# Holding back loads until the second chunk's transpose has landed, in a cross-covariance attention and maxout FFN kernel

## The chip, the cores and the metric

The kernel runs on one core of a Trainium2 chip. The metric is device time in microseconds of that core. A profile's span is some 2 us shorter than the time of the same execution (before: 584.5 of 586.35). GpSimd issues the loads, which cast float32 to bf16 or fp8, into one queue (q0); SyncE issues the DMA transposes and the stores (q1). The profile counts both queues against the same 16 DMA engines. A load or transpose "lands" when its completion is signalled; "the queue is dry" means that no load packet is left to move; "rings" are these queues on the DMA engines. In profile lines PE is TensorE, POOL GpSimd and SP SyncE; v_sb is a v tile, vt_sb its transpose, wo_sb the output weight, h_ps and o_ps what the matmuls for h and for the output write.

## The reference, cut to what matters

```python
# 4 batches; q, k, v: (4, 6144, 256)
qn, kn = q / norm(q, axis=1), k / norm(k, axis=1)
a = softmax(kn.T @ qn / tau)            # 256 x 256 per batch
x = (v @ a).reshape(24576, 256)
h = max(x @ w1, x @ w2, x @ w3)         # 24576 x 768
out = h @ w_out
```

The kernel folds `a` into w1, w2, w3 once per batch, so that each 512-row chunk of v, transposed, needs 36 matmuls for h (128x512) and 24 for the output (128x256). There are 12 chunks per batch, 48 in all, numbered from 0 here; "the second chunk" is chunk 1.

## The kernel before

```python
v_pool = ctx.enter_context(tc.tile_pool(name="v", bufs=5))
...
# issued by GpSimd, in this order, after batch 0's k and q:
load_w(0)
load_v(0)
load_w(1)
load_v(1)
wo_sb = consts.tile([P, FC, d_model], BF16, name="wo_sb")
POOL.dma_start(out=wo_sb, in_=moe_w_out.rearrange("(fc p) d -> p fc d", p=P))
load_v(2)
...
def v_transpose(gi):                    # 256 KB of bf16, through the DMA engines
    v_sb = v_tiles.pop(gi)
    SP.dma_start_transpose(out=vt_tile(gi), in_=v_sb.rearrange("p t c -> p (t c)"))
def v_transpose_pe(gi):                 # the same on TensorE, two copies out of PSUM
    ...
aw_half(et, rinv, aw, 0, [2], lambda: v_transpose_pe(0))
v_transpose(1)

load_v(3)
for b in range(B):
    ...
    for ch in range(NCH):
        gi = b * NCH + ch
        load_v(gi + 4)
        v_transpose(gi + 2)
        if more and 1 <= ch < 9:        # the next batch's k and q, six groups at a time
            load_k(b + 1, (ch - 1) * 6, 6)
            load_q(b + 1, (ch - 1) * 6, 6)
        ...                             # h blocks of this chunk, output of the one before
```

The v tiles have five buffers. Chunk 5's load (v5) takes v0's, and v6 takes v1's: GpSimd must wait with v6 until v1's transpose has read v1. The kernel keeps each engine's instructions in program order (its `keep_order`).

## Time and profile before

| | before |
|---|---|
| time, median | 586.0 us (584.98 to 586.59, 4 runs) |
| span of the profile | 584.5 us |
| TensorE busy | 557.8 us, 95% |
| TensorE's longest wait in chunk work | 4.98 us before chunk 1 |
| granted clock over the span | 0.993 |

The table says that the kernel is a stream of matmuls, with one place in the chunk work where it stops for data. Two groups of the page's list of DMA issues give the normal cost of what is disputed (columns: issues, KB each, median us from issue to landing):

```profile
v_sb<-in_v_dram POOLq DMA_DIRECT2D x48, 256.0 KB, 4.0
...
vt_sb<-v_sb SPq DMA_TRANSPOSE x47, 3.7
```

And GpSimd's timeline shows what it issued behind v1, and where it stopped (start us, length us, what; in brackets its idle time before, and what ended it):

```profile
36.47 0.83 POOL L135 DMA_DIRECT2D wo_sb<-in_moe_w_out_dram  x1 [0.35 <-DMA w_sb<-in_moe_w_dram]
...
42.59 0.53 POOL L102 DMA_DIRECT2D q_sb<-in_q_dram  x1 [0.44 <-DMA w_sb<-in_moe_w_dram]
56.57 0.53 POOL L110 DMA_DIRECT2D v_sb<-in_v_dram  x1 [13.46 <-DMA vt_sb<-v_sb]
```

v6 waited 13.46 us for the transpose of v1.

### The profile page before, as it was taken

Reading aid. Unit: us, or ns where it says so; the run is one execution under the profiler, and the core shown is the slowest. Engines: PE = TensorE matmul, PEld = TensorE weight load, DVE = VectorE, ACT = ScalarE, POOL = GpSimd, SP = SyncE. Lnnn points to the kernel's source line nnn. Section 1 sums busy time; section 2 is a strip of 40 time slices with the busy share of each in tenths; the row PEclk is TensorE's granted clock in tenths of the full one; section 3 lists DMA queues with packets and bytes.
Section 4 is the critical chain, followed back from the end, with each engine's and each line's share of the span. In section 5 each row is a group of like instructions: output and inputs, shape, how many; then the busy total and the mean of one; then the engine's idle time right before and its main releaser. Section 6 shows DMA issues by size and latency. Waiting matters only on the chain.

```text
span 584.5 us, 9286 instructions
## 1 busy us (share of the span) xinstructions
PE 557.8 (95%) x3316; PEld 327.9 (56%) x3316; DVE 405.5 (69%) x623; ACT 305.6 (52%) x526; POOL 225.3 (39%) x232
## 2 busy tenths in 40 slices
PE   2786999999999999999999999999999999999997
PEld 2652555555575555555575555555575555555554
DVE  0035678778748787777848778777857777778775
ACT  0033357676735447767646446767745444444442
POOL 4241017877671006777770105777671000000000
PEclk9998899999999999999999999999999999999999
DMA  8999927988468635888649624899646344323211
GB/s 77 107 171 163 140 56 135 141 122 155 89 118 120 105 101 94 156 131 134 124 87 145 108 83 99 125 155 133 119 91 127 73 90 117 82 58 106 55 72 73
DMA packets 75134, 64.83 MB, mean 111 GB/s; under 512 B 52304, under 2 KB 61392, under 8 KB 75088
## 3 DMA queue, kind: packets, MB, share of 16 engines
q0 software_dynamic: 18400, 26.75, 38.8%
q1 hardware_dynamic: 56544, 37.23, 24.9%
q8 instruction: 26, 0.43, 0.3%
q10 hardware_dynamic: 144, 0.26, 0.1%
q14 instruction: 20, 0.16, 0.1%
HBM read 78.64 MB, written 25.17 MB: 178 GB/s over the span
## 4 chain that ended last, share of the span: by engine, by line
PE 90%; DMA 9%; POOL 1%; issue 0%; DVE 0%; POOLq 0%
PE h_ps L320 63%; PE o_ps L339 21%; DMA q_sb<-in_q_dram 3%; PE gram L226 3%; DMA vt_sb<-v_sb 2%; PE ew_ps L273 2%; DMA k_sb<-in_k_dram 2%; DMA v_sb<-in_v_dram 1%; PE o_ps L359 0%; POOL w_sb L128 0%; POOL k_sb L99 0%; PE n_ps L207 0%; PE n_ps L209 0%; DVE o_sb L365 0%; POOL ident masks.py:199 0%
## 5 line engine op out<-in xcount | busy, mean ns | idle before, releaser
L320 PE MATMUL h_ps<-vt_sb,aw_sb 128*128 128x512 bf16 x1728 | 409.0, 381 | 5.0 <-DMA vt_sb<-v_sb 5.0
L324 DVE TENSOR_TENSOR s_mx<-h_ps,s_mx 128x512 bf16<-128x512 f32 x288 | 197.8, 687 | 105.8 <-ACT s_mx L323 98.7
L320 PEld LDWEIGHTS <-aw_sb 128*128 128x128 bf16 x1728 | 168.8, 98 | 169.9 <-DMA vt_sb<-v_sb 5.5
L323 ACT ACTIVATE s_mx<-h_ps 128x512 bf16<-128x512 f32 x288 | 171.4, 595 | 138.8 <-PE h_ps L320 137.5
L325 DVE TENSOR_TENSOR ht_sb<-h_ps,s_mx 128x512 bf16<-128x512 f32 x288 | 199.3, 692 | 30.7 <-DVE s_mx L324 0.5
L195 POOL TENSOR_TENSOR acc<-acc,sq 128x768 f32<-128x768 f32 x90 | 147.5, 1650 | 70.8 <-ACT sq L189 70.6
L339 PE MATMUL o_ps<-wo_sb,ht_sb 128*128 128x256 bf16 x1128 | 154.0, 273 | 0.0
L339 PEld LDWEIGHTS <-ht_sb 128*128 128x128 bf16 x1128 | 110.5, 98 | 53.3 <-issue 0.6
L342 ACT ACTIVATE o_sb<-o_ps 128x512 f32<-128x512 f32 x94 | 56.1, 597 | 83.0 <-PE o_ps L339 83.0
L110 POOL DMA_DIRECT2D v_sb<-in_v_dram x48 | 26.7, 559 | 105.3 <-DMA vt_sb<-v_sb 101.6
L189 ACT ACTIVATE sq<-q_sb 128x768 bf16<-128x768 fp8e4 x48 | 40.5, 844 | 0.0
L189 ACT ACTIVATE sq<-k_sb 128x768 bf16<-128x768 fp8e4 x48 | 40.1, 835 | 0.0
L192 POOL CAST acc<-sq 128x768 f32<-128x768 bf16 x6 | 4.9, 820 | 74.7 <-ACT sq L189 74.7
L102 POOL DMA_DIRECT2D q_sb<-in_q_dram x32 | 17.6, 553 | 12.4 <-DMA k_sb<-in_k_dram 11.0
L157 PE MATMUL kk<-k_sb 128*128 128x256 fp8e4 x48 | 7.8, 339 | 13.6 <-DMA k_sb<-in_k_dram 13.6
L99 POOL DMA_DIRECT2D k_sb<-in_k_dram x31 | 17.0, 551 | 1.0 <-POOLq L439 0.8
L273 PE MATMUL ew_ps<-w_sb,et 128*128 128x384 bf16 x96 | 17.1, 326 | 0.0
L276 ACT ACTIVATE aw_sb<-ew_ps,rinv 128x384 bf16<-128x384 f32 x24 | 13.8, 581 | 6.1 <-PE ew_ps L273 5.1
L226 PE MATMUL gram<-k_sb,q_sb 128*128 128x512 fp8e4 x144 | 16.8, 276 | 0.0
L226 PEld LDWEIGHTS <-q_sb 128*128 128x256 fp8e4 x144 | 15.9, 136 | 0.6
L178 ACT ACTIVATE lnk<-kb_ps 128x256 f32<-128x256 f32 x1 | 0.4, 384 | 27.6 <-PE kb_ps L175 27.6
L157 PEld LDWEIGHTS <-k_sb 128*128 128x256 fp8e4 x48 | 6.5, 182 | 14.7 <-DMA k_sb<-in_k_dram 14.7
(49 smaller groups left out, 107.7 us busy)
## 6 DMA issues: line engine op xcount, KB each, us to landing
out_dram<-o_sb SPq DMA_DIRECT2D x47, 512.0 KB, 2.9
v_sb<-in_v_dram POOLq DMA_DIRECT2D x48, 256.0 KB, 4.0
k_sb<-in_k_dram POOLq DMA_DIRECT2D x24, 192.0 KB, 5.5
q_sb<-in_q_dram POOLq DMA_DIRECT2D x24, 192.0 KB, 7.0
k_sb<-in_k_dram POOLq DMA_DIRECT2D x5, 256.0 KB, 11.1
q_sb<-in_q_dram POOLq DMA_DIRECT2D x5, 256.0 KB, 19.4
w_sb<-in_moe_w_dram POOLq DMA_DIRECT2D x6, 192.0 KB, 8.9
vt_sb<-v_sb SPq DMA_TRANSPOSE x47, 3.7
```

The costliest lines, as they stand in the source:

```text
L102: POOL.dma_start(out=qk[b][0][:, g0:g0 + w, :], in_=q_r[b][:, g0:g0 + w, :])
L110: POOL.dma_start(out=t, in_=v_r[gi // NCH, gi % NCH])
L189: ACT.activation(out=sq, in_=src, func=AF.Square)
L195: POOL.tensor_tensor(out=acc, in0=acc, in1=sq, op=ALU.add)
L226: PE.matmul(g[:, j * C:(j + 1) * C], lhsT=qt[:, tsl, j * P:(j + 1) * P], rhs=kt[:, tsl, :], start=(tp == 0 and j == 0), stop=(tp == NG // ...
L273: PE.matmul(ew[:, :FH], lhsT=et[:, j, ic * P:(ic + 1) * P], rhs=w_sb[m][:, j, fsl], start=(j == 0), stop=(j == CC - 1))
L320: PE.matmul(t.rearrange("p (t n) -> p t n", t=TPC), lhsT=aw[m][:, ic, fsl], rhs=vt[:, :, ic, :], start=(ic == 0), stop=(ic == CC - 1))
L323: ACT.activation(out=s_mx, in_=hp[0], func=AF.Copy)
L324: DVE.tensor_tensor(out=s_mx, in0=hp[1], in1=s_mx, op=ALU.max)
L325: DVE.tensor_tensor(out=ht[:, fc, :], in0=hp[2], in1=s_mx, op=ALU.max)
L339: PE.matmul(st["ps"][:, half], lhsT=ht[:, fc, t * P:(t + 1) * P], rhs=wo_sb[:, fc, :], start=(fc == 0), stop=(fc == FC - 1))
L342: ACT.activation(out=st["o"][:, t - 1:t + 1, :].rearrange("p t d -> p (t d)"), in_=st["ps"], func=AF.Copy)
```

## The change

Its intent: TensorE waits 5 us for chunk 1's transpose, which shares the DMA engines with loads that nobody needs yet. So those loads are put behind a guard, a one-column copy on GpSimd that reads the transposed tile and so waits for its landing.

```diff
     load_v(1)
     wo_sb = consts.tile([P, FC, d_model], BF16, name="wo_sb")
-    POOL.dma_start(out=wo_sb, in_=moe_w_out.rearrange("(fc p) d -> p fc d", p=P))
-    load_v(2)
...
     v_transpose(1)
+    guard = consts.tile([P, 1], BF16, name="guard")
+    POOL.tensor_copy(out=guard, in_=vts[1][:, TPC - 1, CC - 1, P - 1:P])
+    POOL.dma_start(out=wo_sb, in_=moe_w_out.rearrange("(fc p) d -> p fc d", p=P))
+    load_v(2)
     load_v(3)
```

## The prediction

> **What bounds the kernel now.** I read the page first. TensorE is busy 95% of the 584.5 us span, and the chain that ended last is 90% TensorE and 9% DMA, so the steady part is a matmul stream that loads do not limit. The change touches only the start, so I next read the chain of waits in order of time there, then TensorE's timeline.
>
> The chain of waits, window 0 to 110 us (start us, length us, what):
> ```profile
> 35.54 8.08 DMA v_sb<-in_v_dram
> 43.63 12.41 DMA vt_sb<-v_sb
> 56.09 5.30 PE h_ps L320 x12
> ```
> The second chunk's v load is issued at 35.54 and lands at 43.63. Its transpose, issued then, lands only at 56.05, 12.4 us later. The page gives 3.7 us as the median of all 47 transposes: some 8.7 us are contention.
>
> TensorE, timeline from 44 us:
> ```profile
> 44.47 6.64 PE L320 MATMUL h_ps<-vt_sb,aw_sb 128*128 128x512 bf16 x30
> 56.09 1.46 PE L320 MATMUL h_ps<-vt_sb,aw_sb 128*128 128x512 bf16 x3 [4.98 <-DMA vt_sb<-v_sb]
> ```
> The first chunk ends at 51.11 and TensorE waits 4.98 us. It also comes back slow: 3 matmuls in 1.46 us, where 30 took 6.64. The per-microsecond table shows why (columns: window, length, busy time of PE, PEld, DVE, ACT, POOL, granted clock, DMA share, GB/s):
> ```profile
> 53.00:54.00 1.00, 0.00 (x0) 0.00 (x0) 0.00 (x0) 0.00 (x0) 0.00 (x0) 1.00 1.19 144
> 54.00:55.00 1.00, 0.00 (x0) 0.00 (x0) 0.00 (x0) 0.00 (x0) 0.00 (x0) 0.83 1.55 75
> ...
> 60.00:61.00 1.00, 1.00 (x4) 0.36 (x3) 0.35 (x1) 0.32 (x1) 0.00 (x0) 0.50 1.06 100
> 61.00:62.00 1.00, 1.00 (x8) 0.69 (x7) 0.90 (x2) 0.00 (x0) 0.00 (x0) 0.76 1.03 100
> 62.00:63.00 1.00, 1.00 (x7) 0.48 (x5) 0.14 (x1) 0.38 (x1) 0.00 (x0) 1.00 1.13 109
> ```
> The clock is half from 54.65 (0.83 of one microsecond: 0.65 full, 0.35 half) to 61.5. TensorE works in that state from 56.09 to about 61.48, 5.4 us, and loses half of it: 2.7 us. **The gap costs 4.98 + 2.7 = 7.7 us**, 1.3% of the time. That is all this change can win.
>
> Last, what the rings carried while the transpose waited (q0: loads from GpSimd; q1: SyncE's transposes), window 48 to 49, then 55.5 to 57.5:
> ```profile
> q0 software_dynamic: 94, 0.18, 96.0%
> q1 hardware_dynamic: 95, 0.02, 17.8%
> ```
> ```profile
> q1 hardware_dynamic: 1922, 0.48, 116.1%
> ```
> In company the two queues pass packets one for one, 94 to 95. Alone, the transposes pass 961 a microsecond. A transpose is 256 KB in 256-byte packets, 1024 of them; a v load is 128 packets of 2 KB, a k or q piece 128 of 1.5 KB (from the tile shapes and the trace's packet sizes). So **a transpose needs 1024 load packets to go by, or the load queue to run dry**. Before, it is the latter: the load queue was drained at about 53.6 apart from stragglers, and the transpose landed 2.4 us later.
>
> **What the Trainium skill says.** "DMA: Bandwidth & Descriptors", Queues, rings and completion order: each DMA engine round-robins between the queue rows that have work, at packet granularity. The trace agrees (94 to 95). Same page, Anatomy of one DMA: about 2 us fixed per DMA. The trace agrees in kind: a v load's median is 4.0 us to landing for about 1.3 us of data. "TensorE: Matmul & The Clock Gate", Part 1: after an idle window of about 3.4 us the clock halves; it returns after a busy one; the window runs free. The trace agrees: the half-rate stretch, 54.65 to 61.48, is 6.8 us, two such windows.
>
> **The change, part by part.** No engine's order changes except GpSimd's: one 128x1 copy is added, and the output weight and v2 move behind it.
>
> (a) Removed: no load is issued between v1's (35.54) and the guard. v1 lands at about 43.6 as before, since those loads were behind it in one queue. Its transpose then has free rings: 43.63 + 3.7 = 47.3, before TensorE needs it at 51.11. The 4.98 us gap and its 2.7 us slow stretch go: **-7.7 us**, a kernel of 578.8 if nothing came in their place.
>
> (b) Added: the copy, some 0.2 us (128x1 memsets at the start took 0.10), on an idle GpSimd. Then the output weight is issued at about 47.6.
>
> (c) Moved: the DMA engines fall idle until about 48.9 (issue to first packet was 1.2 us for the v load issued at 56.57). Queued after that, in order: output weight, v2, v3, v4, v5, k, q, v6, k, q. Before, GpSimd stopped ahead of v6 until 56.57, because v6 takes v1's buffer and so waits for v1's transpose. Now that transpose has landed and v6, k, q follow at once. From 46 to 48 only loads ran, at 0.40 MB in 2 us: 1.97 us for the output weight (393 KB) and 1.31 for a v load (262 KB). From 10 to 20, 107 GB/s with fp8 k and q: 1.84 us for 197 KB, about 1.9 beside transposes. Sums: output weight 50.9; v2 52.2; v3, v4, v5 56.1; k, q 59.9; v6 61.2; k, q **65.0**. I add 0.6 for the slow start seen at 58 us.
>
> The output weight lands near 52; its first use, after two blocks of chunk 1 (2 x 1.29 us past 51.11), is 53.7. A thin margin, no wait.
>
> v2 lands at about 53.3 and its transpose is issued then. Ahead of it in time stand v3 to the last q: at most 8 loads x 128 = 1024 packets, fewer once its own first packet has gone out (1.7 us after issue in the steady part, 3.9 under load). So it cannot finish before the queue is dry: 65.6 plus the 2.4 us tail of before, **about 68.0**. Chunk 2 needs it at 51.11 + 36 x 0.216 + 24 x 0.109 = 61.5 (the rates of the chain: 18 in 3.88 us, 6 in 0.66). **A new gap of about 6.5 us, one chunk later.** It is long enough to hold an idle clock window, so the clock halves again: +1.7 to 3.4 us by phase, 2.6 in the middle.
>
> (d) The sum: 586.5 - 7.7 + 6.5 + 2.6 = 587.9. A check by another way: before, chunk 2 began at 67.84 + 1.29 = 69.13; now at 68.0 and 2.6 slower: +1.5, giving 588.0.
>
> **The rivals.**
> 1. *The gap just goes*: v2's transpose is quick or in time, 578.8 to 580. For it: the third and fourth transposes of before were harmless. Against: they had the long gap to finish in, and one for one sharing is what the windows show.
> 2. *The gap moves and shrinks*: the transpose lands at 63 to 66, the clock halves or not by phase, 581 to 586. It needs k, q and v6 to be issued later than I think; nothing but GpSimd's limit of eight loads in flight (the output weight waited for the first weight load, eight before it, by the releasers) holds them, and the last k and q need only the output weight and v2 landed.
> 3. *The gap moves and grows*: slower start, longer tail, transpose at 70, full slow stretch: 590 to 592.
> 4. *The output weight becomes the wait* at 53.7: with 1.7 us of margin at most a microsecond or two, and it would take the same from the later gap, since that one ends at an absolute time.
> GpSimd does not become the bound: it sat idle from 43 to 56.
>
> **Range and chances.** My point is **588.0 us**. 584 to 592 takes in a transpose landing from 65 to 70 and the clock's phase. Even the full gain, 578.8, is 1.3%, so faster by over 2% gets 0.01; slower by over 2% (598.2) needs ten more microseconds than I find: 0.02; within 2%: 0.97.
>
> **What would show it.** Right: vt_sb of the second chunk lands at about 47.3; no TensorE wait near 51; a wait on vt_sb of 5 to 8 us near 61.5; half clock behind it; equal packet counts of both queues between 57 and 65; the next v load (v7) only at about 68. Wrong: no wait at 61.5, more transpose than load packets in company, a wait of the output matmuls on wo_sb at 53.7, or the last k and q issued only after 60.

## The result, and the profile after

The changed kernel takes 587.13 us (586.58 to 587.61, 4 runs) against 586.0. The ratio is 1.0021, interval 1.0001 to 1.0041: within 2%, and slightly slower; a repeat in later rounds gave 1.0024, 1.0011 to 1.0037. Ratios here are the mean time of one kernel's fast runs over that of the other's of the same rounds, so not quite the ratio of the medians.

The chain of waits after, from v1's load on (start us, length us, what):

```profile
35.60 8.07 DMA v_sb<-in_v_dram
43.67 0.02 issue
43.69 2.80 DMA vt_sb<-v_sb
46.49 0.06 issue
46.55 0.19 POOL guard L380
46.73 0.04 issue
46.78 0.82 POOL wo_sb L381
47.60 6.23 DMA v_sb<-in_v_dram
53.83 0.02 issue
53.85 14.24 DMA vt_sb<-v_sb
68.09 0.05 issue
68.13 4.08 PE h_ps L318 x12
```

This is to be read against the three lines of before. Chunk 1's transpose took 2.80 us in place of 12.41: the rings were indeed free. But the chain does not go to TensorE from there. It goes through the guard to v2's load and v2's transpose, and that one took 14.24 us, longer than the one that was cured. TensorE's timeline says the same:

```profile
44.55 9.23 PE L318 MATMUL h_ps<-vt_sb,aw_sb 128*128 128x512 bf16 x42
53.61 0.82 PE L337 MATMUL o_ps<-wo_sb,ht_sb 128*128 128x256 bf16 x6
...
68.13 4.08 PE L318 MATMUL h_ps<-vt_sb,aw_sb 128*128 128x512 bf16 x12 [6.56 <-DMA vt_sb<-v_sb]
```

The 42 h matmuls run from chunk 0 into chunk 1 without a stop, and the output weight, first used at 53.61, is there. Then, one chunk later, TensorE waits 6.56 us. GpSimd's timeline shows that the stop at the v1 buffer has become a stop at v2's, three loads further on:

```profile
50.76 0.60 POOL L110 DMA_DIRECT2D v_sb<-in_v_dram  x1
52.80 0.54 POOL L99 DMA_DIRECT2D k_sb<-in_k_dram  x1 [1.44 <-DMA wo_sb<-in_moe_w_out_dram]
54.12 0.53 POOL L102 DMA_DIRECT2D q_sb<-in_q_dram  x1 [0.78 <-DMA v_sb<-in_v_dram]
68.62 0.53 POOL L110 DMA_DIRECT2D v_sb<-in_v_dram  x1 [13.97 <-DMA vt_sb<-v_sb]
```

The packets of both queues, window 57 to 66 us:

```profile
q0 software_dynamic: 643, 0.95, 96.8%
q1 hardware_dynamic: 588, 0.15, 13.2%
```

In nine microseconds the transposes passed 588 of the 1024 packets that one needs, nearly one for each load packet. From 66.3 on, with the load queue all but dry, they passed 1145 in 1.7 us, those of v3's transpose among them. Sharing is not the whole of the 14.24 us: by the packet records the first transpose packet moved only at 57.68, 3.8 us after the issue, where chunk 1's, with nothing beside it, took 1.3 us (43.69 to 44.97). And the half clock returned, a little shorter in effect than before (columns as in the prediction):

```profile
64.00:65.00 1.00, 0.00 (x0) 0.00 (x0) 0.00 (x0) 0.00 (x0) 0.00 (x0) 0.50 1.12 117
...
69.00:70.00 1.00, 1.00 (x4) 0.42 (x3) 0.00 (x0) 0.60 (x1) 1.00 (x3) 0.50 1.10 339
70.00:71.00 1.00, 1.00 (x5) 0.33 (x3) 0.77 (x2) 0.00 (x0) 0.21 (x1) 0.58 1.30 224
71.00:72.00 1.00, 1.00 (x6) 0.46 (x5) 0.62 (x1) 0.60 (x1) 0.00 (x0) 1.00 1.19 141
```

The clock is back at about 70.8, so TensorE works 2.7 us at half speed, and loses 1.3 us (before: 5.4 and 2.7). The account: before lost 4.98 + 2.7 = 7.7 us, after loses 6.56 + 1.3 = 7.9. That fits the two profiled executions, 584.5 and 584.8 us; the medians are 1.1 us apart, and the other executions of the two were not traced.

### The profile page after: what moved, and what is told of

Its sections match the earlier page's. It is cut to its first block, busy times and chain, and to the rows that moved or that the text cites. A ratio compares the mean times of both kernels' runs of the same rounds, so it can differ in the third digit from the quotient of the medians.

```text
span 584.8 us, 9287 instructions
## 1 busy us (share of the span) xinstructions
PE 556.3 (95%) x3316; PEld 327.3 (56%) x3316; DVE 405.4 (69%) x623; ACT 305.6 (52%) x526; POOL 225.7 (39%) x233
## 4 chain that ended last, share of the span: by engine, by line
PE 88%; DMA 10%; POOL 1%; issue 0%; DVE 0%; POOLq 0%
PE h_ps L318 61%; PE o_ps L337 21%; DMA q_sb<-in_q_dram 3%; DMA vt_sb<-v_sb 3%; PE gram L224 3%; DMA v_sb<-in_v_dram 2%; PE ew_ps L271 2%; DMA k_sb<-in_k_dram 2%; PE o_ps L357 0%; POOL w_sb L128 0%; POOL k_sb L99 0%; PE n_ps L205 0%; PE n_ps L207 0%; POOL wo_sb L381 0%; DVE o_sb L363 0%
```

## The experiments

The theory: once its first packet moves, a transpose passes one packet for each load packet, so it lands only when enough load packets have gone by or the load queue is dry; the guard merely moved the transpose that meets the full queue. The rivals: v2's transpose is late because v2 was issued late; or the output weight is what matters in either gap. All kernels give the right result. Unless it says otherwise, an edit is to the changed kernel.

### Two by two: which of the two moved loads matters

Either load goes back in front of the guard alone, then both do.

```diff
 e1_wo_before                       e2_v2_before
     wo_sb = consts.tile(...)           wo_sb = consts.tile(...)
+    POOL.dma_start(out=wo_sb, ...) +   load_v(2)
     ...                                ...
     POOL.tensor_copy(out=guard, ...)   POOL.tensor_copy(out=guard, ...)
-    POOL.dma_start(out=wo_sb, ...)     POOL.dma_start(out=wo_sb, ...)
     load_v(2)                      -   load_v(2)
     load_v(3)                          load_v(3)

 e3_guard_before_v3: both edits, so only load_v(3) and later stay behind the guard
```

> Only v2 and later loads stay behind the guard; the output weight goes back in front. Theory (the new wait at chunk 2 comes from the loads queued behind v2, packet for packet): the output weight has passed before the second chunk's transpose starts, which still lands by 47.5 us; the load queue is dry some 2 us sooner than in the changed kernel, v2's transpose lands at about 66, the gap before chunk 2 is 4 to 5 us instead of 6.6: 584 to 586 us. Rival (holding back the output weight is what counts in either gap): the first gap of 5 us comes back, or the second goes: 579 or 586 with a wait near 51.

Measured: 586.01 us (584.38 to 586.27), ratio to before 0.9995. In the profile chunk 1 had no wait, v2's transpose took 14.42 us and landed at 65.81, and the gap before chunk 2 was 4.46 us. The place of the output weight shifts the gap by about the 2 us that the weight's own load takes, and does not make or cure it. The profiled execution was the quickest of four; the others, at 586.0 to 586.3, had a granted clock of 0.993 against its 0.995, which fits a longer half-rate stretch; they were not traced.

> Only the output weight and v3 and later stay behind the guard; v2 goes in front. Theory: v2's transpose follows the first one directly and both land by 51 us, no wait before chunk 1 or 2; the third chunk's transpose now stands against the queue (output weight to the k and q behind v7) and lands near 72, when it is needed: gap of 0 to 1 us, 578.5 to 580. Rival (any load issued close behind v1 slows its transpose as before): a wait of 2 us or more near 51, above 582.

Measured: 580.07 us (578.76 to 580.52), ratio 0.9896, just above my range. No wait before chunk 1 or 2; what is left is 1.05 us before chunk 3, at 72.99, and 0.19 us for the output weight at 53.58. The guard still holds that weight, which landed 7.1 us after its issue here (5.7 in the changed kernel).

> Output weight and v2 both back in front, the guard alone stays, ahead of v3. Theory: 56 load packets per engine more behind v1 have passed by 46 us, both transposes land by 51, v3's near 70, before 72: no wait on a transpose at all, 578.5 to 579.5, better than both kernels. Rival (the output weight and v2 behind v1 made the first gap): wait of several us near 51, 583 or more.

Measured: 579.46 us (579.25 to 579.5), ratio 0.9888, interval 0.9874 to 0.9903. The output weight and v2 right behind v1, which the change had taken for the culprits, did chunk 1's transpose little harm: it landed at 47.99, 4.24 us after its issue. So most of the 12.41 us of before came from v3 and the loads after it. Here are v3's own transpose, from the chain of waits, and TensorE's one wait on a transpose in this profile, where I had expected none:

```profile
54.16 18.20 DMA vt_sb<-v_sb
...
72.41 2.76 PE L320 MATMUL h_ps<-vt_sb,aw_sb 128*128 128x512 bf16 x12 [0.40 <-DMA vt_sb<-v_sb]
```

v3's transpose took 18.20 us, longer than the one that was cured, but it was needed only at about 72: the contention is still there, moved to where there is time for it.

So what matters is on which side of the guard v2 stands: with it behind, some 586 to 587 us; in front, 579 to 580. The output weight's place is worth about 1 us. The rival about the output weight falls. But v2 in front is also v2 early, so these three do not yet tell the queue from the late issue.

### A second guard: does a free ring for v2's transpose cure it?

```diff
     load_v(2)
+    v_transpose(2)
+    guard2 = consts.tile([P, 1], BF16, name="guard2")
+    POOL.tensor_copy(out=guard2, in_=vts[2][:, TPC - 1, CC - 1, P - 1:P])
     load_v(3)
...
-            v_transpose(gi + 2)
+            if gi > 0:
+                v_transpose(gi + 2)
```

> The changed kernel with a second guard: v3 and later wait for v2's transpose as well. Theory: v2's transpose lands near 57 and chunk 2 starts without a wait, but v3 then starts at 57, its transpose stands against v4 to the k and q behind v7 and lands near 78, needed at 72: the gap moves on to chunk 3, 5 to 7 us, 584 to 588. Rival (v2's transpose was late because v2 was; a free ring for it is the cure): no gap left, 579.

Measured: 589.22 us (588.47 to 590.49), ratio 1.0058, the slowest of all. The chain of waits from chunk 1's transpose on:

```profile
43.82 3.15 DMA vt_sb<-v_sb
...
53.71 3.10 DMA vt_sb<-v_sb
...
60.67 19.49 DMA vt_sb<-v_sb
80.17 0.05 issue
80.21 3.88 PE h_ps L318 x9
```

This is the cleanest picture of the mechanism. Two guards make two transposes quick, 3.15 and 3.10 us, and the next, the first without one, takes 19.49. v2 was issued at 48.08, no earlier than in the changed kernel (47.60), and its transpose was quick and in time: the rival about v2's late issue falls. The gap went on to chunk 3, at 8.13 us rather than the 5 to 7 that I expected, and the time came 1 us above my range; I had taken the transpose to land near 78, and it landed at 80.16.

### A shorter queue, and smaller packets

```diff
 e5_kq_later
-            if more and 1 <= ch < 9:
-                load_k(b + 1, (ch - 1) * 6, 6)
-                load_q(b + 1, (ch - 1) * 6, 6)
+            if more and 2 <= ch < 10:
+                load_k(b + 1, (ch - 2) * 6, 6)
+                load_q(b + 1, (ch - 2) * 6, 6)

 e8_small_packets: the first two pieces of k and of q take every second group of twelve
-                load_k(b + 1, (ch - 1) * 6, 6)
-                load_q(b + 1, (ch - 1) * 6, 6)
+                if gi < 3:
+                    for i, src in ((1, k_r), (0, q_r)):
+                        POOL.dma_start(
+                            out=qk[1][i][:, 0:12, :].rearrange("p (h t) c -> t p h c", t=2)[ch - 1],
+                            in_=src[1][:, 0:12, :].rearrange("p (h t) c -> t p h c", t=2)[ch - 1])
+                else:
+                    load_k(b + 1, (ch - 1) * 6, 6)
+                    load_q(b + 1, (ch - 1) * 6, 6)
```

> The changed kernel with the next batch's k and q loads begun one chunk later, which takes one k and one q piece (256 packets, some 4 us of the queue) out of the loads ahead of the stop at v7. Theory: v2's load lands as before at about 53.9, its transpose 4 us sooner, at about 64; gap before chunk 2 of 2.5 us, no half clock: 581 to 583. Rival (the lateness comes from v2's own late issue): the transpose and the time stay, 587.

Measured: 583.49 us (582.79 to 586.2), ratio 0.9966. v2 landed at 53.95 as before, its transpose took 11.56 us in place of 14.24, and the gap was 3.65 us with the clock whole in the profile. The direction is the theory's; the size is not. I expected the transpose 4 us sooner and it was 2.7, and the median is 0.5 us above my range. The packet records tell a part of it: the load queue ran nearly dry at about 62.7 in place of 66.3, 3.6 us sooner, but with less company to pass in, the transpose had passed only some 260 packets by 62 (588 by 66 in the changed kernel), and had the rest to do alone. Alone need not be fast: from 63 to 64.7 the DMA engines moved 57 GB/s, where the transposes of before had moved 238 (55.5 to 57.5). What holds the last packets back no run shows. One of the four runs, at 586.2, had a clock of 0.994 against 0.998 of the profiled one: a gap of about that length may halve the clock in one execution and not in the next, but that run was not traced.

> The changed kernel with the first two k and q pieces of the next batch cut otherwise: every second group of twelve, same bytes, 768 packets of 256 bytes in place of 128 of 1536. Theory (the transpose passes one packet for each load packet, so the number of load packets decides): from about 57 us it needs 64 load packets per engine, which now take about 4 us, so v2's transpose lands at 61.5 to 63.5 with the load queue still full; gap before chunk 2 of 0 to 2 us, no half clock: 579 to 582. Rival (the transpose needs the load queue to run dry, or gets a share of the bytes or time): it lands at 68 or later, 587 or more.

Measured: the profiled execution took 581.62 us, with a gap of 2.34 us and a whole clock; three more took 584.62 to 585.43 at a clock of 0.996 to 0.997 against its 0.999. The median is 584.93, ratio 0.9960: outside my range, and the three were not traced. Their lower clock is worth some 1.5 us (an estimate: 0.0025 of 582) of the 3.0 to 3.8 by which they were slower; the rest stays unexplained. The question it was made for is answered by the trace all the same. v2's transpose landed at 64.42, a microsecond later than I had it:

```profile
54.29 10.13 DMA vt_sb<-v_sb
```

And at 60 to 62 us, in its midst, the two queues passed

```profile
q0 software_dynamic: 478, 0.12, 88.0%
q1 hardware_dynamic: 477, 0.12, 46.2%
```

one for one again, with packets of 256 bytes on both sides. The load queue had work until 73. So the transpose does not need the queue to run dry, and it is not given a fixed share of bytes: it needs about as many load packets to pass as it has itself, and small ones pass sooner. From 58.1 to 62.81 its 1024 went by (1040 of the transposes' queue), beside 1158 load packets; in the second-guard kernel the transpose of 19.49 us passed its own beside 1041, from 65 to 79.5. In the profiled execution, the same bytes of k and q in 768 packets per piece in place of 128 brought the landing forward by 3.7 us.

### The clock measured by itself

```diff
+            if gi == 2:
+                fill_ps = htile("fill_ps")
+                for i in range(28):
+                    PE.matmul(fill_ps, lhsT=ident, rhs=warm, start=(i == 0), stop=(i == 27))
             for fc in range(FC):
                 h_block(gi, aw, fc)
```

> The changed kernel with 28 idle matmuls (28 x 0.216 = 6.0 us) put before chunk 2, inside the gap. Theory: the transpose lands as before at about 68.1, so the gap stays, but the clock isn't halved and the 12 matmuls after it take 2.6 us instead of 3.9: 1.3 us less than the changed kernel, 585.8. Rival (the gap's length alone counts, or the fill delays chunk 2): 587 or more.

> The changed kernel again, beside the others on one chip: 587 us, gap of 6.6 us before chunk 2, half clock for two idle windows (6.8 us) of which TensorE works in 2.5 to 4 by the window's phase.

Measured: 585.53 us (584.72 to 586.08) against 587.35 (586.74 to 588.11) for the changed kernel in the same rounds; the means differ by 1.9 us. In the profile the transpose landed at 68.22, as without the fill, and the 12 matmuls behind the gap were at full speed:

```profile
61.66 6.21 PE L416 MATMUL fill_ps<-warm,ident 128*128 128x512 bf16 x27
68.26 2.76 PE L318 MATMUL h_ps<-vt_sb,aw_sb 128*128 128x512 bf16 x12 [0.39 <-DMA vt_sb<-v_sb]
```

2.76 us in place of 4.08: the clock's share is 1.3 us in these profiles, 1.9 over five runs. The repeat of the changed kernel had a gap of 5.97 us and much the same 4.12 us for the 12 matmuls, but a half-rate stretch of one window, 67.51 to 70.92, where I had expected two.

### Versions that beat both kernels

`e6_pe_transpose` is the kernel before with no guard; chunk 1 is transposed by TensorE in chunk 0's fourth block.

```diff
-    v_transpose(1)
...
+            if gi == 0:
+                gaps[3].append(lambda: v_transpose_pe(1))
```

> The kernel before, without any guard, with the second chunk transposed by TensorE inside chunk 0 (eight 128x128 transposes, two copies). Theory: no transpose stands against the queue before v2's, which starts at about 47 and, with v6, k, q now free to follow, lands near 60.5, needed at 62: no wait of over 0.5 us, the price is 0.6 us of TensorE: 579 to 580.5. Rival (TensorE stalls on the copies, or v2's transpose is late): 582 or more.

Measured: 579.23 us (579.15 to 579.42), ratio 0.9885. The eight TensorE transposes took 0.45 us of the chain, and TensorE had no wait on a transpose. The path was not quite the expected one: GpSimd stood before v6 for 13.52 us all the same, until v2's transpose had landed at 56.07, not near 60.5; v6, k and q did not follow at once, and why the profile doesn't show.

`e9_v3_guard_kq_later` joins the guard ahead of v3 with the later k and q.

> The guard ahead of v3 and the next batch's k and q one chunk later, together. Theory: the 0.4 us wait left before chunk 3 with the guard ahead of v3 goes, as the queue before that transpose is one k and one q piece shorter: 579.0 to 579.4, the same as the TensorE transpose within 0.3 us. Rival (something else holds the start): no change from 579.5, or later k and q make the squares wait and it is slower.

Measured: 579.15 us (578.96 to 579.33), ratio 0.9873, interval 0.9854 to 0.9891. No wait on a transpose is left. Its median and that of the TensorE transpose are 0.1 us apart, though taken on different chips, and both are within 0.5 us of the 578.8 that the prediction worked out for a kernel without the gap.

## Why the prediction was right

- **The bound and the size at stake, 7.7 us: right, a little high.** The versions without the gap save 6.8 us against the before of their own rounds (585.98 to 579.23), and 7.1 (586.29 to 579.15).
- **Part (a), the first gap goes: right.** Chunk 1's transpose landed at 46.49; I had 47.3, from the page's median of 3.7 us, and with nothing beside it, it took 2.80.
- **Part (b), the guard: right,** 0.19 us against 0.2.
- **Part (c), the gap moves to chunk 2: right, with its sum.** The load queue was nearly dry at 66.3 (65.6 predicted), the transpose landed at 68.09 (68.0), the gap was 6.56 us (6.5), v7 was issued at 68.62 (about 68). The output weight was there at its first use, 53.61. That the landing came within 0.1 us is in part luck: the queue ran dry 0.7 us later than predicted, and the tail after it took 1.8 us in place of the 2.4 taken over from before. Why there is a tail was not known then and isn't now. That the loads queued behind v2 are the cause was argued then and is shown now, by the second guard, the shorter queue and the smaller packets.
- **One for one sharing: right,** 588 to 643 from 57 to 66, and 477 to 478 with small packets. "Or the load queue to run dry" was the case here; the small packets and the second guard show the other branch.
- **The clock, 2.6 us: mis-sized.** It cost 1.3 us in the profile, under the low end of my 1.7 to 3.4, and 1.9 by the filled gap. I took the middle, as if the half-rate stretch began anywhere; here it began 2.4 us into a gap of 6.56 us, and most of it, 64.0 to 68.13 of 64.0 to 70.8, passed while TensorE was idle. With 1.3 in place of 2.6 the sum of 587.9 becomes 586.6, and the profiled execution took 586.68.
- **"Within 2%" was next to certain:** the prediction says itself that even the full gain is 1.3%. What was at risk were the waits and their times.
- **Rival 2 (moved and shrunk) and rival 3 (moved and grown)** were sizes of the same story; the first is what the shorter queue made of it, the second what the second guard made. Rival 1 falls with the 6.56 us wait, rival 4 with the output matmuls that did not wait.

What stays open: e8's three slower runs, which carry a lower clock but no trace; why a transpose beside loads starts late (first packet after 3.8 us in place of 1.3) and ends slowly (the tail after the queue is dry); and why the start of the whole sequence moves by up to a microsecond from run to run (v1's landing was at 43.3 to 44.3 in these profiles).

## What to carry to other kernels

Before holding back loads for the sake of one transfer, ask which transfer will stand in front of the held-back pile: a barrier in a load queue moves contention to the next unguarded consumer and can make it worse if it also lets a buffer wait go, as v6's did (issued at 50.76 in place of 56.57). Count packets, not only bytes, where two queues share the DMA engines as here, and put the barrier behind everything that is needed next (here behind v2, not ahead of it), or take the urgent transfer off the engines altogether. An idle matmul engine can pay twice, in the gap and in the slow clock after it: here it did in every traced gap of 4.46 us and more in the chunk work.

## What the Trainium skill lacked or had wrong

- "DMA: Bandwidth & Descriptors", Queues, rings and completion order: the round robin by packet agrees with the traces, whose packet records pass one for one (477 to 478); whether such a record is what the page calls a packet, 9 to 17 descriptors as a rule, no run shows. What it lacks is the consequence for a DMA transpose, whose packets here are 256 bytes: beside loads of 1.5 and 2 KB packets, a transpose of 256 KB took 11.6 to 19.5 us where it stood in the chain of waits, against 2.80 alone.
- The same page, Rules for kernel authors, in its row on two DMA transposes from different queues, says that "A transpose next to ordinary DMAs needs nothing". The row is about corrupted data, and there it agrees (all results were right); for time it doesn't hold: a transpose beside loads took 12.4 us in place of 2.80 here.
- The same page, Rules for kernel authors, counsels coalescing many small transfers into a large one. No run here changed the number of transfers; what the page lacks is that the packets within one matter to a neighbour: in one profiled execution the same bytes in six times as many packets let a transpose beside them land 3.7 us sooner (64.42 against 68.09).
- No page tells how late the first packet of a transpose moves beside loads: 3.8 us after the issue here, against 1.3 alone.
- "TensorE: Matmul & The Clock Gate", Part 1: a window of about 3.4 us that runs free agrees with the runs. The gaps of 4.46 us and more that were traced in the chunk work halved the clock, one of 3.65 us did not; the stretch at half rate lasted one window or two (3.4 us and 6.8 us), and 6.2 us of idle matmuls prevented it. But the window need not be idle throughout, and how idle it must be the page does not say. In the changed kernel the clock halved at 64.01, and the 3.41 us before that, from 60.60, still held matmuls until 61.57, 0.97 us. In its repeat the window before, 60.68 to 64.10 (counted back from the halving at 67.51), held 1.49 us of them, and the clock stayed whole at its end.
